# Sparse attention scores of two batches from f16 halves in 64x32 tiles of the array

## The chip, the cores and the metric

One core of one Trainium2 chip runs the whole kernel in one launch. The metric is device time in microseconds (us), the median of the runs shown; lower is better.

## The reference, cut to what matters

Block-sparse attention over 4 batches of 8 heads (768 rows, head size 64, blocks of 32 rows), then one feed-forward layer on the 3072 x 512 result:

```python
scores = np.matmul(q, k.transpose(0, 1, 3, 2)) / np.sqrt(64)
mask = (abs(blk_i - blk_j) <= 1) | first block | last block (rows and columns alike)
mask |= the 3 sampled key blocks of each query block
attn = softmax(np.where(mask, scores, -1e9))
x = np.matmul(attn, v)                      # then (3072, 512)
h = x @ w_in                                # 512 x 2048
out = (h * erf(softplus(h))) @ w_out        # 2048 x 512
```

A middle query block sees at most 8 key blocks of 32: its three neighbours, three sampled ones, the first and the last. The first and the last query block see all 24.

## The kernel before, in words

Everything is arranged around one loop of 96 feed-forward groups (line 985), eight to a chunk of 256 rows. A group on TensorE is 24 matmuls for `h` (`ff_first`) and 12 for `o` (`ff_second`, two groups late); its activation is five ScalarE passes (`ff_logs`), a VectorE step (`ff_power`), one more ScalarE pass (`ff_exp`), and three VectorE steps that also make f16 halves (`ff_gate`, in the next step).

The attention of later rows is laid between the groups: 64 **units**, 16 to a batch, at most one to a step, in five or six of every eight steps (`until`, line 984). Of a batch's units ten are "m" (four middle query blocks of four heads), four are "f" (the first and last query block against all keys, two heads each), and two "e" (the two query blocks left over). With n the number of a unit in its batch, n = 0 to 9 are the m units. A unit takes `scores` on TensorE, `soft_max` on VectorE (a maximum per row and group), `soft_exp` on ScalarE (four exponentials, one f16 copy), `soft_low` on VectorE (the lower f16 half), and `soft_turn` (transposes by DMA, from the SP queue). Two units later `values` multiplies by V on TensorE in 128x32 tiles of the array, `norm` divides on VectorE, and for every second unit `turn` makes halves of x.

Each engine works in the order in which the program issues (`InOrder`, line 49). Within a step that is: h of this group; its ScalarE logs; values; gathers; scores; gate of the last group; norm; o; the row maximum; the next queries; power; exponentials; stores; turn; the low half and the transposes; then `behind` (line 822), the preparation of the next batch. The score tile has one buffer, `h` three.

Scores now are f32 for all batches. A head pair's queries are laid into `qm` with zeros, so that 128 rows of the array hold two heads; each query block is a 64-column tile. `scores` (line 568) makes, for an m unit, four matmuls of the end keys (64 columns, 128-column tiles, two query blocks at once) and eight of near and sampled keys (192 columns, 64-column tiles). TensorE runs every f32 matmul as two instructions.

Preparation of batch b+1 in `behind`: keys are loaded (`load_k`, n = 0, 2, 4, 6) and laid into blocks by GpSimd (`order_k`, n = 1, 3, 5, 7); values are loaded, squared on ScalarE (n = 2, 4), scaled by a power of two (n = 5), split into f16 halves by ScalarE and VectorE (n = 5, 6, 8, 9) and written to a table in DRAM, from which SP gathers blocks. Key blocks of the sampled numbers are gathered by GpSimd copies (`gather`). Queries are laid out by two VectorE copies (`order_q`, n odd).

Of the kernel before, what the change touches and what calls it, by code (L numbers as in the profile page):

```python
# [42 lines left out]
def sparse_attention_moe(ctx: ExitStack, tc: tile.TileContext, qT, kT, v, sampled, w_in, w_out, out):  # L43
# [56 lines left out]


    NKEY = 2 * (NB + 1)
    keys = cp.tile([P, NKEY + KGS * NR, HP * BLOCK], F32, tag="keys", name="keys")
    kring = iter(range(B * NM))

    def key_blocks(b):
        return keys[:, b % 2 * (NB + 1) : (b % 2 + 1) * (NB + 1)]

    samp2 = at.tile([P, NB, NR, 2], I32, tag="xf", name="samp2", bufs=1)
# [4 lines left out]
    def load_k(b, pr):  # L114

        if b == 0:
            if pr < 3:
                kr = at.tile([P, 1024], F32, tag="pT", name=f"kr_{b}_{pr}", bufs=3)[:, :S]
            else:
                kr = at.tile([P, KT * 2 * VW], F16, tag="vn", name=f"kr_{b}_{pr}", bufs=1).bitcast(F32)[:, :S]  # L120
        else:
            kr = wi[:, NK * NG :, :].rearrange("p n c -> p (n c)")[:, :S]
        sp.dma_start(kr, kT[b, 2 * pr : 2 * pr + 2].rearrange("t d s -> (t d) s"))
        krs[b, pr] = kr
# [8 lines left out]


    qts = {}
    qm = cp.tile([P, HP, 4, 2, BLOCK], F32, tag="qm", name="qm")
    pool.memset(qm, 0.0)

# [12 lines left out]
    def order_q(b, t):  # L151
        qt = qts.pop((b, t)).rearrange("p r (j c) -> p r j c", c=BLOCK)
        copy = act.copy if b == 0 and t in (1, 2) else dve.tensor_copy
        for a in range(2):
            copy(qm[a * D : (a + 1) * D, :, :, a, :], qt[a * D : (a + 1) * D])

    QW = 4 * VW
# [47 lines left out]
    def pow2_scale(whole, tag):  # L205

        m = st.tile([P, 1], F32, tag="m", name=f"m_{tag}", bufs=1)
        dve.tensor_scalar_max(m, whole, 1e-37)
        e = st.tile([P, 1], I32, tag="e", name=f"e_{tag}", bufs=1)
        dve.tensor_scalar(e, m.bitcast(I32), 24, None, ALU.logical_shift_right)  # L210
        s = st.tile([P, 1], F32, tag="s_" + tag[:2], name=f"s_{tag}", bufs=1)
        inv = st.tile([P, 1], F32, tag="i_" + tag[:2], name=f"i_{tag}", bufs=1)
# [3 lines left out]
        return s, inv  # L216

# [188 lines left out]

    def weight_tile(name, n):
        return cp.tile([P, n + 2, 512], F32, tag=name, name=name)

    NG = DFF // 512  # L410
    wi = weight_tile("wi", NK * NG)
    wo = weight_tile("wo", NF)
    wi16 = wi.rearrange("p n c -> p (n c)").bitcast(F16).rearrange("p (n c) -> p n c", c=1024)
# [99 lines left out]
    def soft_max(unit):  # L513

        s, groups, width = softs[unit]
        tag = "_".join(str(x) for x in unit)
        mx = st.tile([P, 4], F32, tag="mx", name=f"mx_{tag}")[:, :groups]
        dve.reduce_max(mx, s.rearrange("p (g w) -> p g w", w=width), AX.X)
        nb = st.tile([P, 4], F32, tag="nb", name=f"nb_{tag}")[:, :groups]
        dve.tensor_scalar(nb, mx, -1.0 / math.sqrt(D), P_SHIFT * math.log(2.0), ALU.mult, ALU.add)  # L520
        softs[unit] += (nb,)

    def soft_exp(unit):
# [3 lines left out]
        n = groups * width  # L527
        pf = at.tile([P, 1024], F32, tag="pf", name=f"pf_{tag}", bufs=1)[:, :n]
        for g in range(groups):
            c = slice(g * width, (g + 1) * width)  # L530
            act.activation(pf[:, c], s[:, c], AF.Exp, bias=nb[:, g : g + 1], scale=1.0 / math.sqrt(D))
        p2 = at.tile([P, 2048], F16, tag="p2", name=f"p2_{tag}", bufs=2)[:, : 2 * n]
# [33 lines left out]
    pts = {}  # L566

    def scores(unit):
        kind, b, n = unit[0], unit[1], unit[2:]
        tag = "_".join(str(x) for x in unit)  # L570
        s = ps_s.tile([P, 1024], F32, tag="s", name=f"s_{tag}")
        if kind == "m":
# [15 lines left out]
        elif kind == "e":  # L588
            (quad,) = n
            s3 = s.rearrange("p (r w) -> p r w", r=HP)  # L590
            for r in range(2):
                pr = 2 * quad + r
                q_ = qm[:, pr, :2].rearrange("p j a c -> p (j a c)")
                pe.matmul(s3[:, r, 192:], q_, end_keys(b, pr), start=True, stop=True)
                for j in range(2):
# [16 lines left out]
    def values(b, t, quad):  # L612
        po = ps_po.tile([P, 4, D + 1], F32, tag="po", name=f"po_{b}_{t}_{quad}")
        for hl in range(4):
# [5 lines left out]
            for x, ln in ((0, 0), (0, 1), (1, 0)):  # L620
                for half in range(2):
                    for j in range(4):
                        if t < MT:
                            pT = pts["m", b, t, quad][:, ((j // 2) * 2 + r) * 4 + x * 2 + half]
                            col = (j % 2) * 64 + a * 32
                            vg = vb[:, slot_of[b, 1 + 4 * t + j]]
                        elif j in (1, 2):
                            pT, col = pts["e", b, quad][:, r * 4 + x * 2 + half], (j - 1) * 64 + a * 32
                            vg = vb[:, slot_of[b, NB - 4 + j]]
# [4 lines left out]
                if t == MT:  # L634
                    for k in range(KT):
                        for j in (0, 3):
                            pT, col = pts["f", b, pr][:, x * KT + k], (0 if j else 64) + a * 32
                            w = slice(c, c + D + 1) if ln == 0 else slice(c + D + 2, c + VW)
# [172 lines left out]
    def next_queries(m):  # L811

        b, n = divmod(m, per)
        if n < 10 and n % 2 == 1:
            order_q(b, n // 2 + 1)
            if n < 9:
                load_q(b, n // 2 + 2)
        if n == per - 1 and b + 1 < B:
            order_q(b + 1, 0)
            load_q(b + 1, 1)  # L820

    def behind(m):

        b, n = divmod(m, per)
        if b + 1 < B:
            c = b + 1
            if n == 10:
                load_q(c, 0)
            k = n if b else 2 * (n - 10) if n > 9 else -1
            if k in ((1, 3, 5, 7) if b else (2, 4, 6, 8)):  # L830
                order_k(c, (k - 1) // 2)
            if k in (0, 2, 4, 6):
                load_k(c, k // 2)
            if k == 8:
                have_k.add(c)
            if b == 0:
                n -= 4
            if n in (1, 7):
                load_v(c, 0)
            if n == 3:  # L840
                load_v(c, 1)
            if n in (2, 4):
                square_v(c, n // 2 - 1)
            if n == 5:
                scale_v(c)
            if n in (5, 6):
                split_v(c, 1, n - 5)
            if n in (8, 9):
                split_v(c, 0, n - 8)
            if n == 9:  # L850
                have_v.add(c)

# [228 lines left out]
```

## Time and profile before

| | us |
|---|---|
| median of 3 runs | 847.46 (846.92, 847.46, 854.24) |
| the profiled execution | 845.28 |
| its span, first to last instruction | 843.5 |
| TensorE busy | 742.9 (88%) |
| ScalarE busy | 601.3 (71%) |
| VectorE busy | 554.4 (66%) |
| GpSimd busy | 125.9 (15%) |
| mean granted TensorE clock | 0.939 of 2.4 GHz |

In the names of the profile, PE is TensorE, PEld its weight loads, ACT ScalarE, DVE VectorE, POOL GpSimd, SPq the queue of DMAs that SyncE issues. All instructions go through one helper and so bear one line number; they are told apart by tile names: `s_m`, `s_f`, `s_e` are the scores of the three kinds, `pf` and `p` their exponentials and f16 halves, `pT` the transposed halves, `po` the product with the values, `vn` the f16 halves of the values, `vj` the squares of the values.

### The profile page before, as it was taken

How to read it: one execution, taken by the hardware profiler on the slowest of the kernel's cores; microseconds unless marked ns; L12 is line 12 of the kernel's file. 1: busy time of each engine (PE TensorE's matmuls, PEld its weight loads, DVE VectorE, ACT ScalarE, POOL GpSimd, SP SyncE). 2: the span in 40 equal slices, each digit the busy share in tenths (PEclk: the TensorE clock that was granted, in tenths of full speed). 3: DMA queues.
4: the chain of work that ended last, by engine and by line, in shares of the span. 5: the costliest groups of instructions: out<-in, count | busy, mean ns of one | idle time of the engine just before them, and what ended most of it. 6: DMA issues, size and time to landing. Idle time of an engine off the chain costs nothing.

```text
span 843.5 us, 24600 instructions
## 1 busy us (share of the span) xinstructions
PE 742.9 (88%) x10044; PEld 513.2 (61%) x10044; DVE 554.4 (66%) x977; ACT 601.3 (71%) x999; POOL 125.9 (15%) x344
## 2 busy tenths in 40 slices
PE   1364647899999999989999999999999999999997
PEld 1253424666666676656777666566676776666664
DVE  3985696887665766755667676757576767655454
ACT  4654657987766777866778777868577777777774
POOL 5521111001222221000202221000111100000000
PEclk9865867989989999999999999999999999999999
DMA  8999853797788687741597798633476858111000
GB/s 326 269 276 317 220 138 78 171 208 171 178 220 205 185 206 201 185 89 44 135 218 186 198 194 189 161 84 82 106 175 175 175 109 196 39 32 40 1 26 26
DMA packets 199922, 131.48 MB, mean 156 GB/s; under 512 B 144000, under 2 KB 167168, under 8 KB 199808
## 3 DMA queue, kind: packets, MB, share of 16 engines
q1 hardware_dynamic: 196384, 118.10, 57.3%
q0 software_dynamic: 3424, 11.80, 4.1%
q8 instruction: 79, 1.29, 0.6%
q14 instruction: 35, 0.29, 0.1%
HBM read 83.88 MB, written 12.95 MB: 115 GB/s over the span
## 4 chain that ended last, share of the span: by engine, by line
PE 47%; DVE 19%; DMA 13%; ACT 12%; issue 5%; SPq 3%; POOL 0%; ACTq 0%; POOLq 0%
PE h L59 18%; PE o L59 17%; PE s_m L59 6%; DMA vb<-vtab 5%; PE po L59 3%; DVE g L59 3%; DVE q L59 3%; DMA vtab<-vn 3%; SPq L59 3%; DVE mx_m L59 3%; ACT x L59 3%; DMA vraw<-in_v_dram 3%; ACT pf_m L59 2%; ACT q L59 2%; DVE p_m L59 2%
## 5 line engine op out<-in xcount | busy, mean ns | idle before, releaser
L59 PE MATMUL h<-xT,wi 128*128 128x256 f16 x2304 | 274.9, 277 | 12.4 <-ACT wi L59 5.4
L59 PE MATMUL o<-wo,g 128*128 128x512 f16 x1152 | 270.5, 385 | 4.0 <-ACT wo L59 2.3
L59 PEld LDWEIGHTS <-wi 128*128 128x128 f16 x2304 | 227.7, 99 | 64.1 <-ACT wi L59 6.7
L59 PEld LDWEIGHTS <-g 128*128 128x128 f16 x1152 | 110.5, 99 | 138.2 <-issue 22.1
L59 ACT ACTIVATE x<-x 128x512 f32<-128x512 f32 x288 | 181.5, 630 | 9.2
L59 POOL COPY keys<-keys 128x128 f32 x264 | 92.9, 404 | 296.6 <-PE s_m L59 190.1
L59 PE MATMUL s_m<-keys,qm 128*64 128x192 f32 (+1 forms) x960 | 117.1, 344 | 4.5 <-ACT pf_m L59 3.7
L59 ACT ACTIVATE pf_m<-s_m,nb_m 128x256 f32<-128x256 f32 x160 | 62.8, 475 | 70.4 <-DVE nb_m L59 65.5
L59 DVE SCALAR_TENSOR_TENSOR q<-x,q 128x512 f32<-128x512 f32 x96 | 66.8, 696 | 62.5 <-ACT x L59 61.2
L59 PEld LDWEIGHTS s_m<-keys,qm 128*64 128x64 f32 (+1 forms) x960 | 90.9, 171 | 18.4 <-ACT pf_m L59 4.7
L59 ACT ACTIVATE x<-h,isg 128x512 f32<-128x512 f32 x96 | 65.3, 680 | 40.7 <-PE h L59 40.3
L59 ACT ACTIVATE q<-q 128x512 f32<-128x512 f32 x96 | 59.5, 619 | 29.8 <-DVE q L59 29.8
L59 DVE SCALAR_TENSOR_TENSOR q<-q,h 128x512 f32<-128x512 f32 x96 | 65.5, 682 | 22.6 <-ACT q L59 21.9
L59 DVE TENSOR_TENSOR p_m<-pf_m,p_m 128x1024 f16<-128x1024 f32 x40 | 49.1, 1228 | 32.3 <-ACT p_m L59 32.3
L59 DVE SCALAR_TENSOR_TENSOR g<-q,g 128x512 f16<-128x512 f32 x96 | 67.1, 699 | 3.3
L59 DVE TENSOR_REDUCE mx_m<-s_m 128x4 f32<-128x1024 f32 x40 | 48.8, 1220 | 31.1 <-PE s_m L59 31.1
L59 ACT ACTIVATE q<-x 128x512 f32<-128x512 f32 x96 | 60.5, 630 | 3.0
L59 PE MATMUL po<-vb,pT_m 128*32 128x65 f16 (+1 forms) x3840 | 44.1, 203 | 16.7 <-DMA vb<-vtab 10.2
L59 PEld LDWEIGHTS <-pT_m 128*32 128x32 f16 x3840 | 37.7, 99 | 27.7 <-DMA vb<-vtab 11.7
L59 DVE TENSOR_TENSOR x<-xf,x 128x512 f16<-128x512 f32 x24 | 16.9, 703 | 42.8 <-ACT x L59 42.8
L59 DVE TENSOR_SCALAR g<-q 128x512 f16<-128x512 f32 x96 | 41.5, 433 | 3.3
L59 ACT ACTIVATE p_m<-pf_m 128x1024 f16<-128x1024 f32 x40 | 42.3, 1057 | 1.3
(111 smaller groups left out, 544.1 us busy)
## 6 DMA issues: line engine op xcount, KB each, us to landing
vb<-vtab SPq DMA_DIRECT2D x280, 65.0 KB, 2.8
vb<-vtab SPq DMA_DIRECT2D x32, 390.0 KB, 4.0
vraw<-in_v_dram SPq DMA_DIRECT2D x10, 768.0 KB, 5.0
vtab<-vn SPq DMA_DIRECT2D x16, 390.0 KB, 4.9
vb<-vtab SPq DMA_DIRECT2D x12, 520.0 KB, 5.0
qt<-in_qT_dram SPq DMA_DIRECT2D x20, 256.0 KB, 3.7
out_dram<-wo SPq DMA_DIRECT2D x20, 256.0 KB, 3.5
vb<-vtab SPq DMA_DIRECT2D x36, 130.0 KB, 2.9
```

Source lines behind the costliest of these rows:

```text
L59: done = call(*args, **kwargs)
```

## The change

For batches 0 and 1 one thing differs: the end keys are multiplied block by block, eight matmuls in 64-column tiles in place of four in 128-column tiles (likewise in the e units).

For batches 2 and 3 keys and queries are scaled by a power of two, taken from the sum of their squares, and split into two f16 halves, which take the room of the f32 value. A score is the sum of three products, high by high, high by low and low by high. There are no zeros any more: the two heads of a pair lie in the two row halves of the array. The near and sampled keys of an m unit are 48 matmuls of 192 columns in 64x32 tiles, the end keys 12 of 64 columns in 64x128 tiles; an f unit is 12 matmuls in 64x64 tiles, an e unit 12 and 24. The two heads of an m or e unit are 512 columns apart in the score tile, those of an f unit lie in the same columns of the two partition halves.

The preparation of batches 2 and 3 (in `behind`, during batches 1 and 2) changes: keys and queries are first loaded raw and squared on ScalarE (eight squares, five more loads), a scale is made, keys are loaded again and split by ScalarE and VectorE (n = 5 to 8) where GpSimd laid them out; queries are split by ScalarE and VectorE in place of two VectorE copies. The steps for the values move to later n. Preparation of batch 1 stays as it was (`behind_whole`).

```diff
+    def split_k(b, pr):
+        ...
+        hi, lo = kx[:, :NB, 0, c], kx[:, :NB, 1, c]
+        act.activation(hi, kr, AF.Copy, scale=s)
+        dve.scalar_tensor_tensor(lo, kr, s, hi, ALU.mult, ALU.subtract)
+        if pr == HP - 1:
+            pool.tensor_copy(key_blocks(b)[:, NB], key_blocks(b)[:, 0])
+    def raw_k(b, pr):
+        sp.dma_start(spare_wi, kT[b, 2 * pr : 2 * pr + 2].rearrange("t d s -> (t d) s"))
+    def raw_two(b, key, pr):
+        place = ld.tile([P, H // 2, KT * D], F32, tag="vraw", name=f"{key}raw_{b}_{pr}", bufs=1)
+        ...
+        sp.dma_start(place, x[b, 2 * pr : 2 * pr + 4].rearrange("(r t) d s -> (t d) r s", t=2))
+    def square_raw(b, key, pr):
+        ...
+        act.activation(junk, raws.pop((b, key, pr)), AF.Square, accum_out=qksq[b][:, n : n + 1])
+    def bound_qk(b):
+        dve.tensor_reduce(top, qksq.pop(b).rearrange("p (x n) -> p x n", n=HP), AX.X, ALU.add)
+    def scale_qk(b):
+        pe.matmul(whole, one.to_broadcast([P, P]), qktop.pop(b), start=True, stop=True)
+        qkscale[b] = pow2_scale(whole, f"q{b}")
+        ...
+    def split_q(b, t):
+        hi, lo = qh[:, t % 2, 0], qh[:, t % 2, 1]
+        act.activation(hi, qt, AF.Copy, scale=s)
+        dve.scalar_tensor_tensor(lo, qt, s, hi, ALU.mult, ALU.subtract)
...
+    THREE = ((0, 0), (0, 1), (1, 0))
+    def half_products(outs):
+        for n, (x, y) in enumerate(THREE):
+            for out, a, lhs, rhs in outs:
+                rows = slice(a * D, (a + 1) * D)
+                pe.matmul(out, lhs(rows, x), rhs(rows, y), start=n == 0, stop=n == 2)
+    def half_scores(unit):
+        ...
+        if kind == "f":
+            for c, e in ((0, 512), (512, S)):
+                half_products([(s[a * D : (a + 1) * D, c:e], a, ...) for a in range(2)])
+        ...
+        for r, o, out in turns:
+            half_products([(out[o : o + whole, a, 192:256], a, ...) for a in range(2)])
+        for r, o, out in turns:
+            for j in range(blocks):
+                for a in range(2):
+                    place = out[o + c : o + c + BLOCK, a, :192]
+                    outs.append((place, a, queries(pr, c, c + BLOCK), keys_near(first + j, pr)))
+            half_products(outs)
     def scores(unit):
+        if b >= FB:
+            half_scores(unit)
+            return
...
-                for g in range(2):
-                    q_ = qm[:, pr, 2 * g : 2 * g + 2].rearrange("p j a c -> p (j a c)")
-                    pe.matmul(s4[:, g, r, 192:], q_, end_keys(b, pr), start=True, stop=True)
+                for j in range(4):
+                    o = slice((j % 2) * 64, (j % 2) * 64 + 64)
+                    q_ = qm[:, pr, j].rearrange("p a c -> p (a c)")
+                    pe.matmul(s4[o, j // 2, r, 192:], q_, end_keys(b, pr), start=True, stop=True)
...
     def behind(m):
         if b + 1 < B:
             c = b + 1
+            if c < FB:
+                behind_whole(c, b, n)
+                return
+            if n == 0:
+                raw_k(c, 0)
+                raw_two(c, "k", 1)
+            if n == 1:
+                for pr in range(3):
+                    square_raw(c, "k", pr)
+                raw_k(c, 3)
+                raw_two(c, "q", 0)
+            if n == 2:
+                square_raw(c, "k", 3)
+                square_raw(c, "q", 0)
+                square_raw(c, "q", 1)
+                load_k(c, 0)
+                raw_two(c, "q", 2)
+            if n == 3:
+                square_raw(c, "q", 2)
+                square_raw(c, "q", 3)
+                bound_qk(c)
                 load_v(c, 0)
+            if n == 4:
+                scale_qk(c)
+                square_v(c, 0)
                 load_v(c, 1)
             if n == 5:
+                square_v(c, 1)
+            if 5 <= n < 9:
+                split_k(c, n - 5)
+                if n < 8:
+                    load_k(c, n - 4)
+            if n == 6:
                 scale_v(c)
+            if n in (6, 7):
+                split_v(c, 1, n - 6)
+            if n == 7:
+                load_v(c, 0)
             if n in (8, 9):
                 split_v(c, 0, n - 8)
```

## Rows read from the trace of the kernel before

**Rows 1.** The page, part 1: busy time and share of the span.

```profile
PE 742.9 (88%) x10044; PEld 513.2 (61%) x10044; DVE 554.4 (66%) x977; ACT 601.3 (71%) x999; POOL 125.9 (15%) x344
```

**Rows 2.** Busy time by stage: length, PE, PEld, DVE, ACT, POOL, clock, DMA, GB/s.

```profile
216.50:322.80 106.30, 101.71 (x1516) 72.02 (x1515) 67.75 (x125) 75.07 (x132) 25.26 (x68) 0.95 0.82 200
395.00:508.00 113.00, 110.88 (x1624) 78.93 (x1622) 75.07 (x136) 86.27 (x150) 22.49 (x59) 1.00 0.76 185
573.80:687.00 113.20, 111.66 (x1622) 79.30 (x1621) 73.60 (x130) 83.59 (x142) 15.15 (x48) 0.98 0.66 146
```

**Rows 3.** TensorE's timeline, one unit step of batch 3 (start, length, ..., count).

```profile
627.84 2.78 PE L59 MATMUL h<-xT,wi 128*128 128x256 f16 x24
630.56 0.96 PE L59 MATMUL po<-vb,pT_m 128*32 128x65 f16 x96
631.44 2.56 PE L59 MATMUL s_m<-keys,qm 128*128 128x64 f32 x24
633.93 2.76 PE L59 MATMUL o<-wo,g 128*128 128x512 f16 x12
636.53 2.78 PE L59 MATMUL h<-xT,wi 128*128 128x256 f16 x24
```

**Rows 4.** The chain of waits, an f and an e unit of batch 2.

```profile
542.59 1.29 PE s_f L59 x4
...
557.87 1.68 PE s_e L59 x12
```

**Rows 5.** VectorE's and ScalarE's timelines between neighbouring units of batch 3.

```profile
638.26 1.23 DVE L59 TENSOR_TENSOR p_m<-pf_m,p_m 128x1024 f16<-128x1024 f32 x1 [2.19 <-ACT p_m L59]
642.76 1.23 DVE L59 TENSOR_REDUCE mx_m<-s_m 128x4 f32<-128x1024 f32 x1 [0.75 <-PE s_m L59]
...
639.35 0.69 ACT L59 ACTIVATE x<-h,isg 128x512 f32<-128x512 f32 x1 [0.61 <-PE h L59]
642.06 0.63 ACT L59 ACTIVATE x<-x 128x512 f32<-128x512 f32 x1
645.93 1.06 ACT L59 ACTIVATE p_m<-pf_m 128x1024 f16<-128x1024 f32 x1
```

**Rows 6.** ScalarE's timeline in batch 2: units n = 1, 2, then 7, 8.

```profile
418.69 1.06 ACT L59 ACTIVATE p_m<-pf_m 128x1024 f16<-128x1024 f32 x1
428.20 1.06 ACT L59 ACTIVATE p_m<-pf_m 128x1024 f16<-128x1024 f32 x1
...
491.16 1.06 ACT L59 ACTIVATE p_m<-pf_m 128x1024 f16<-128x1024 f32 x1
504.03 1.06 ACT L59 ACTIVATE p_m<-pf_m 128x1024 f16<-128x1024 f32 x1
509.25 1.12 ACT L59 ACTIVATE vn<-vraw,s_v 128x384 f16<-128x384 f32 x2 [3.65 <-issue]
```

**Rows 7.** The tile p_m in batch 3: count, first and last start.

```profile
L59 ACT ACTIVATE p_m<-pf_m x10: 1056/1057/1057, 582.0 to 696.2; 128x1024 f16<-128x1024 f32 x10
```

**Rows 8.** Groups by shape: total busy us, mean ns of one.

```profile
L59 ACT ACTIVATE vj<-vraw 128x768 bf16<-128x768 f32 x14 | 11.7, 835 | 1.3 <-DMA vraw<-in_v_dram 1.2
L59 ACT ACTIVATION_READ_ACCUMULATOR vj<-vraw 128x1 f32 x14 | 2.6, 186 | 0.0
L59 DVE SCALAR_TENSOR_TENSOR vn<-vraw,s_v,vn 128x384 f16<-128x384 f32 x28 | 16.1, 620 | 16.1 <-ACT vn L59 16.1
L59 DVE SCALAR_TENSOR_TENSOR wi<-wi,s_wi 128x1024 f16<-128x1024 f32 x8 | 10.4, 1303 | 1.9 <-ACT wi L59 1.9
```

**Rows 9.** ScalarE's waits, 446 to 508 us: total, times, longest.

```profile
ACT vn L59 <- DVE i_v L59: 2.4, 1, 2.4
```

**Rows 10.** SP's queue, batch 3: one gather of value blocks.

```profile
632.73 7.19 SPq L59 DMA_DIRECT2D vb<-vtab  x14
```

**Rows 11.** TensorE's timeline where it stood still in batch 3.

```profile
593.02 0.37 PE L59 MATMUL po<-vb,pT_f 128*32 128x64 f16 x13 [1.54 <-issue]
593.33 3.81 PE L59 MATMUL s_m<-keys,qm 128*128 128x64 f32 x24
```

More of the change, by code (lines that the diff above doesn't have):

```diff
@@ new lines, in half_scores, with queries, keys_at, keys_near @@
+    def half_scores(unit):
+        kind, b, n = unit[0], unit[1], unit[2:]
+        tag = "_".join(str(x) for x in unit)
+        s = ps_s.tile([P, 1024], F32, tag="s", name=f"s_{tag}")
+        t = n[0] if kind == "m" else MT
+        q = qh[:, t % 2]
+        base = b % 2 * (NB + 1)
+        def queries(pr, c, e):
+            return lambda rows, x: q[rows, x, pr, c:e]
+        def keys_at(first, last, pr, step=1):
+            c = slice(pr * BLOCK, (pr + 1) * BLOCK)
+            return lambda rows, x: halves_of_keys[rows, base + first : base + last : step, x, c]
+        def keys_near(i, pr):
+            return lambda rows, x: half_near(rows, b, i, pr, x)
+        if kind == "f":
+            (pr,) = n
+            for c, e in ((0, 512), (512, S)):
+                half_products(
+                    [
+                        (s[a * D : (a + 1) * D, c:e], a, queries(pr, 2 * BLOCK, P), keys_at(c // BLOCK, e // BLOCK, pr))
+                        for a in range(2)
+                    ]
+                )
+            softs[unit] = (s[:, :S], 1, S)
+            return
+        if kind == "m":
+            quad = n[1]
+            s4 = s.rearrange("p (a r w) -> p a r w", a=2, r=2)
+            first, blocks, turns = 1 + 4 * t, 4, [(r, 0, s4[:, :, r]) for r in range(2)]
+            softs[unit] = (s, 4, 256)
+        else:
+            (quad,) = n
+            s3 = s.rearrange("p (a w) -> p a w", a=2)[:, :, :256]
+            first, blocks, turns = NB - 3, 2, [(r, r * D, s3) for r in range(2)]
+            softs[unit] = (s3, 2, 256)
+        whole = blocks * BLOCK
+        for r, o, out in turns:
+            pr = 2 * quad + r
+            half_products(
+                [
+                    (out[o : o + whole, a, 192:256], a, queries(pr, 0, whole), keys_at(0, NB, pr, NB - 1))
+                    for a in range(2)
+                ]
+            )
+        for r, o, out in turns:
+            pr = 2 * quad + r
+            outs = []
+            for j in range(blocks):
+                c = j * BLOCK
+                for a in range(2):
+                    place = out[o + c : o + c + BLOCK, a, :192]
+                    outs.append((place, a, queries(pr, c, c + BLOCK), keys_near(first + j, pr)))
+            half_products(outs)
@@ L592, in scores @@
                 pr = 2 * quad + r
-                q_ = qm[:, pr, :2].rearrange("p j a c -> p (j a c)")
-                pe.matmul(s3[:, r, 192:], q_, end_keys(b, pr), start=True, stop=True)
+                for j in range(2):
+                    o = slice(j * 64, j * 64 + 64)
+                    q_ = qm[:, pr, j].rearrange("p a c -> p (a c)")
+                    pe.matmul(s3[o, r, 192:], q_, end_keys(b, pr), start=True, stop=True)
                 for j in range(2):
@@ L850, in behind @@
             if n == 9:
+                have_k.add(c)
                 have_v.add(c)
```

124 lines of the change are left out of this document (89 added, 35 removed).

## The prediction

> **What bounds the kernel now.** I read the page first: TensorE is busy 88% of the span, the next engine 71% [rows 1]. A share over the whole says little, so the second view is busy time by stage, over the m units of batches 1, 2 and 3 [rows 2]: TensorE is busy 96% to 99% of each, ScalarE 71% to 76%, VectorE 64% to 66%. By this view TensorE is the bound, and the reader is tempted to take off what the change takes off TensorE.
>
> The third view, the timelines, shows what comes next. TensorE takes 8.69 us for a step with a unit: 2.72 for h, 0.88 for the values, 2.49 for the scores, 2.60 for o [rows 3]. A step without a unit is two stretches of 6144 columns, 2.60 each: 5.20. Beside it runs a loop through VectorE and ScalarE: lower half of unit n, gate, division, maximum of unit n+1 (VectorE), four exponentials and the f16 copy (ScalarE), then the lower half again. Between neighbouring units it took 8.73, from 638.26 to the end of the copy at 646.99, and in it VectorE waited for the scores 0.75 [rows 5]. The loop alone is thus 8.0: it lies 0.7 below TensorE's 8.69. With a step without a unit between, the copies of n = 7 and 8 end 12.87 apart [rows 6], against TensorE's 8.69 + 5.20 = 13.89. With the turning of x between neighbours, n = 1 to 2, it is 9.51 [rows 6], already above TensorE's 8.69. So TensorE may become faster by about 0.7 to 1.0 per unit before the loop is the bound, and what lengthens the loop costs at once.
>
> **What TensorE saves.** The f unit streams 768 columns in 1.29 [rows 4]: 1.68 ns a column in f32, against 2.60 / 6144 = 0.42 in f16 [rows 3]. An e unit has half of an m unit's matmuls but four changes of tile shape where m has two: 2 x 1.68 - 2.49 = 0.87 is six changes, 0.15 each [rows 3, 4]. Of the m unit's 2.49, near keys are 8 x 192 x 1.68 ns, two at once, 1.29; changes 0.30; end keys the remaining 0.90.
>
> After, in batches 2 and 3: the 48 near matmuls run in six sets of eight tiles, 192 x 0.42 = 81 ns a set, 0.48. For the end keys the nearest row is the values, 96 matmuls of 65 columns in four tiles in 0.88 [rows 3]: 37 ns a set, six sets 0.22. With two changes, 1.00, so 1.49 saved. No row shows tiles in row halves. Bounds: at the values' pace of 9.2 ns per matmul the unit is 60 x 9.2 ns + 0.30 = 0.85; with the two row halves one after the other it is 1.71. I take 1.00, since the values' four tiles already run side by side. An e unit is 0.48 + 0.22 + 0.30 = 1.00, saving 0.68; an f unit 3 x 768 x 0.42 ns + 0.15 = 1.12, saving 0.17, or at the other bound 2.09, costing 0.80. Per batch 14.9 + 1.4 + 0.7 = 17, for two 34.
>
> On f the Trainium skill speaks against the change: TensorEngine Tiling (Array Packing), Gotcha 1: PSUM Pressure, says that different row tiles cannot access the same PSUM bank at once. The f unit's two heads go to the same columns; by that rule it takes the 2.09, and the sum rises by 8 x 0.97 = 7.8. No row here shows it either way.
>
> In batches 0 and 1 the end keys become 16 instructions of half the tile width, two at once as the near keys are: half of 0.90, and one change fewer, 0.60 saved per m unit, 0.67 per e unit (three changes and half of its 0.45), 7.3 per batch. If the weight loads don't run side by side it is only the changes, 0.15 and 0.45. In all TensorE sheds up to 49.
>
> The same skill has a second rule against it: TensorE: Matmul & The Clock Gate, in the section on the 56 ns, gives 25 ns as the least from one matmul's start to the next. By it the m unit would be 60 x 25 ns + 0.30 = 1.80. The values' 9.2 ns [rows 3] contradict that floor for tiles side by side, so I keep 1.00; by 1.80 the sum would rise by about 5, since the loop hides the rest.
>
> **What the loop gives back.** Batch 3 has no preparation behind it. Its ten copies lie 114.2 apart from first to last [rows 7]. By the loop: neighbours 9.5 + 8.0 + 8.0, six with a free step at 12.9, and 1.6 for a double set of values (0.9) and a store on ScalarE (0.7): 104.5. The standstill of 1.54 and the slower scores behind it, 3.81 against 2.56 [rows 3, 11], come on top if they stay: 107.3. Saved 7 to 10, I take 8; the f and e units save their 2.0: **-10**.
>
> In batches 1 and 2 ScalarE and VectorE prepare the next batch. A square is 0.835 + 0.186 = 1.02; a split on ScalarE the same 0.84; the lower half of 768 columns lies between 0.62 for 384 and 1.30 for 1024, 1.03 [rows 8]. Between two copies ScalarE has the last exponential, 0.5, and the logs, 3.3 (639.35 to 642.69), and VectorE 5.3 up to the maximum's end [rows 5]; ScalarE thus has 1.4 free between neighbours, and none with a free step between, where logs and power lie on the path. Step by step in batch 2, against now:
> - n = 0: TensorE binds here, two sets of values: -1.5.
> - n = 1: three squares and the turn's copy: 0.5 + 0.6 + 3.1 + 3.3 = 7.5 against VectorE's 9.5 - 2.7 = 6.8: +0.7.
> - n = 2: three squares for two of the values, a free step behind: +1.0. n = 3: two squares, likewise: +2.0. n = 4: the scale, three more one-column steps at 0.19 (the shortest row): +0.5.
> - n = 5: the wait of 2.4 for the values' scale [rows 9] and a split of 1.2 go, two squares and a split come: -0.5. n = 6: that wait comes here, covered in part, with a lower half of 1.03: +2.2. n = 7: lower halves of 1.03 and 2 x 0.62 where there were none: +2.3. n = 8: one more lower half, but the wait of 3.65 for the values' load [rows 6] shrinks, as the steps before it are longer: -1.5.
>
> That is +5.2; f and e units save 2.0: **+3**. In batch 1 six units follow each other without a free step, where ScalarE's 1.4 hides n = 3 wholly, and n = 0 saves 0.6: +4.1, less 1.3 for e: **+3**. Batch 0 is bound by the start; of its 7.3 I take **-2** (ends 0 and -7).
>
> Queries: two VectorE copies become one ScalarE and one VectorE pass beside the exponentials, nothing. GpSimd loses the laying out of keys; behind it waited nobody for long, nothing. Five more loads per batch stand on SP's queue ahead of the next gathers: 7.19 / 14 = 0.51 per issue [rows 10], 5 in all; between nothing and 5 I take **+2**. Cover for it is the two units between transposition and values.
>
> Sum: -10 + 3 + 3 - 2 + 2 = -4 against the profiled 845.3, 841.3. The median of the runs shown lies 2.2 above that execution: **843**.
>
> **Rivals.**
> TensorE is the only bound, the loop adjusts: 845.3 - 49 + 2.2 = 798. For it 96% to 99% busy; against it the 8.0, 9.51 and 12.87. Chance 0.10.
>
> The preparation hides: ScalarE is idle 31 and 27 in these stages of batches 1 and 2 [rows 2], the additions vanish, and their TensorE gains show for a third of 16.9 and 7.3: -10 - 6 - 2 - 2 = -20, 828. Against it the order on each engine: idle time lies ahead of the exponentials, the squares behind them. Chance 0.15.
>
> Slower: the raw loads come late. Each is issued behind a unit's transposes, and, where its place holds earlier data, behind the squares of that; one step later ScalarE stands at its square, with the logs, the exponentials, and so h's and the score tile's buffers behind it. The wait of 3.65 for the values [rows 6] is this mechanism. Ten such waits (n = 1 to 5, two batches), each 3.65 less 1.4 free, are 22: 865. It decides from six of the ten on, 13 above forecast. For it SP's issues back to back, 7.19 [rows 10]; against it most of the steps are 9 to 15 long. Chance 0.20.
>
> f's row halves exclude each other (the bound of 2.09): 843 + 6 = 849, since most of the f units lie where TensorE binds. Chance 0.05.
>
> The change not doing what it says, no tiles side by side: excluded by the values' row, within 0.02.
>
> **Numbers.** The forecast has 0.48; its own range is 833 to 853, a quarter of it below 839. A measurement of this kernel can tell about 1%, 8 us, from no change. Faster by more: 0.10 + 0.15 + 0.12 = 0.37. Slower by more: 0.20 and the 0.02 = 0.22. Within: 0.41. The range, 820 to 862, leaves out the first rival and the upper half of the third.
>
> **What would show it.** Right: scores of an m unit near 1.0, TensorE's busy share in batch 2's m units fallen to some 85%, the row maximum no longer waiting for scores, copies of neighbours 8.0 apart in batch 3, n = 6 and 7 of batches 1 and 2 over 2 longer. Wrong: ScalarE waiting for raw loads; an f unit of 2.1; neighbours under 8; or a TensorE that now stands still so often that its granted clock falls more than in [rows 2], each fall costing what the 3.81 shows [rows 11].

## The result, and the profile after

The changed kernel took 856.21 us (median of 18 runs, 850.69 to 862.82) against 847.38 of the kernel before: a ratio of 1.0097, 95% interval 1.0073 to 1.0121. It is slower by about 8 us where 843 and "no change that can be told" were forecast. The profiled execution took 852.04, its span is 850.0, four below the median.

Part 1 and part 4 of the page after:

```profile
PE 703.6 (83%) x11104; PEld 475.2 (56%) x11104; DVE 561.8 (66%) x987; ACT 636.2 (75%) x1051; POOL 117.6 (14%) x330
...
PE 33%; DVE 22%; ACT 21%; DMA 14%; issue 7%; SPq 2%; POOL 1%; ACTq 0%; POOLq 0%; DVEq 0%
```

TensorE has 39 us less to do than in [rows 1], and the kernel is slower. Its share of the chain that ended last is 33%, where it was 47% before.

Stages, cut at the ends of the f16 copies of n = 0 and n = 9 of each batch, show where (us, worked out from the starts of `p_m` in the timelines; the first stage is from the start to batch 1's n = 0, "f, e" runs to the next batch's n = 0):

| | start | m, batch 1 | f, e | m, batch 2 | f, e | m, batch 3 | rest |
|---|---|---|---|---|---|---|---|
| before | 225.8 | 111.6 | 67.0 | 117.4 | 61.4 | 114.2 | 146.2 |
| after | 230.6 | 118.8 | 60.0 | 128.8 | 59.6 | 107.5 | 144.6 |
| `ends_only` | 226.8 | 112.8 | 59.7 | 116.9 | 61.6 | 111.6 | 149.0 |
| `fixed_scale` | 229.3 | 115.7 | 61.1 | 120.7 | 58.7 | 108.2 | 144.5 |
| `no_loads` | 226.8 | 117.1 | 59.5 | 121.5 | 58.6 | 107.0 | 144.4 |

Batch 3 gains, as forecast; batch 2 loses 11.4 where 5.2 was forecast. Up to batch 1's n = 0 after and `ends_only` issue the same instructions, so of the 4.8 at the start 3.8 lie between executions, not in the program. The 67.0 of before is long for a reason of its own: TensorE stood 2.2 there without a semaphore, and its granted clock was 1.2 GHz from 376.0 to 382.8; after and `ends_only` have neither in that stage.

TensorE's timeline of unit steps in batch 3 after (start, length, ..., count), against [rows 3]:

```profile
637.39 2.78 PE L59 MATMUL h<-xT,wi 128*128 128x256 f16 x24
640.10 1.08 PE L59 MATMUL po<-vb,pT_m 128*32 128x65 f16 x96
641.12 0.97 PE L59 MATMUL s_m<-keys,qm 64*128 64x64 f16 x60
642.02 2.76 PE L59 MATMUL o<-wo,g 128*128 128x512 f16 x12
644.62 2.78 PE L59 MATMUL h<-xT,wi 128*128 128x256 f16 x24
```

From the scores' start to o's is 0.90, against 2.49 before. An f and an e unit in the chain after, against 1.29 and 1.68 of [rows 4]:

```profile
558.22 1.09 PE s_f L59 x12
...
573.60 0.63 PE s_e L59 x36
```

The stages of the m units of batches 1, 2 and 3 after (columns as in [rows 2]):

```profile
221.20:340.00 118.80, 102.41 (x1639) 71.25 (x1641) 75.61 (x141) 88.86 (x159) 21.82 (x62) 0.91 0.89 215
398.00:527.00 129.00, 112.41 (x2015) 74.13 (x2017) 82.03 (x149) 106.28 (x182) 17.82 (x52) 0.92 0.82 192
577.00:685.00 108.00, 98.75 (x1821) 67.62 (x1819) 72.43 (x124) 87.41 (x144) 14.96 (x48) 1.00 0.62 140
```

In batch 1's stage the DMA engines are at 0.89 and TensorE's granted clock at 0.91; in batch 2's 0.82 and 0.92. In batch 3's, where nothing is prepared, 0.62 and 1.00. ScalarE's timeline of the copies of batch 2, n = 0 to 8:

```profile
408.34 1.06 ACT L59 ACTIVATE p_m<-pf_m 128x1024 f16<-128x1024 f32 x1
427.98 1.06 ACT L59 ACTIVATE p_m<-pf_m 128x1024 f16<-128x1024 f32 x1
437.92 1.06 ACT L59 ACTIVATE p_m<-pf_m 128x1024 f16<-128x1024 f32 x1
453.45 1.06 ACT L59 ACTIVATE p_m<-pf_m 128x1024 f16<-128x1024 f32 x1
468.06 1.06 ACT L59 ACTIVATE p_m<-pf_m 128x1024 f16<-128x1024 f32 x1
477.29 1.06 ACT L59 ACTIVATE p_m<-pf_m 128x1024 f16<-128x1024 f32 x1
493.29 1.06 ACT L59 ACTIVATE p_m<-pf_m 128x1024 f16<-128x1024 f32 x1
505.96 1.06 ACT L59 ACTIVATE p_m<-pf_m 128x1024 f16<-128x1024 f32 x1
521.40 1.06 ACT L59 ACTIVATE p_m<-pf_m 128x1024 f16<-128x1024 f32 x1
```

| from n to n + 1 | 0 | 1 | 2 | 3 | 4 | 5 | 6 | 7 | 8 |
|---|---|---|---|---|---|---|---|---|---|
| before | 15.37 | 9.51 | 14.74 | 12.98 | 9.12 | 16.48 | 9.64 | 12.87 | 16.64 |
| after | 19.64 | 9.94 | 15.53 | 14.61 | 9.23 | 16.00 | 12.67 | 15.44 | 15.77 |
| difference | +4.3 | +0.4 | +0.8 | +1.6 | +0.1 | -0.5 | +3.0 | +2.6 | -0.9 |
| forecast | -1.5 | +0.7 | +1.0 | +2.0 | +0.5 | -0.5 | +2.2 | +2.3 | -1.5 |

From n = 1 on the steps of the preparation cost what was forecast, within 0.8 each. The step from n = 0 to 1 is the one that came out far off: TensorE was to save 1.5 there, and 4.3 were lost. Its timeline and three stretches of it (columns as before):

```profile
416.17 0.19 PE L59 MATMUL po<-vb,pT_e 128*32 128x64 f16 x2
421.83 0.90 PE L59 MATMUL po<-vb,pT_f 128*32 128x65 f16 x25
422.66 1.59 PE L59 MATMUL s_m<-keys,qm 64*128 64x64 f16 x60
424.19 3.75 PE L59 MATMUL o<-wo,g 128*128 128x512 f16 x12
```

```profile
416.30:419.40 3.10, 0.20 (x23) 0.07 (x8) 0.69 (x1) 2.55 (x5) 0.00 (x0) 1.00 0.99 327
419.40:421.80 2.40, 0.00 (x0) 0.00 (x0) 0.00 (x0) 0.00 (x0) 0.00 (x0) 0.50 0.11 33
421.80:426.20 4.40, 4.38 (x93) 2.61 (x94) 2.57 (x6) 0.19 (x1) 1.79 (x8) 0.50 0.54 156
```

In the middle of the values' product TensorE stands for 5.5 us. No semaphore holds it; VectorE does little in it, and in its last 2.4 us none of the engines listed does anything. The granted clock is at half, 1.2 GHz, from 419.4 to 426.2, and the scores take 1.59 where they take 0.97. A raw load of batch 3's keys was issued just before, the second of the tile `kraw`:

```profile
L59 SPq DMA_DIRECT2D kraw<-in_kT_dram x2: 420/429/438, 235.1 to 412.8; - x2
...
DMA to landing us min/median/max: 5.4/5.9/6.5
```

Issued at 412.8, it landed at 419.3, within the standstill; until then the DMA engines were 0.99 busy, after it 0.11. That is a suspicion, and the experiments are on it.

### The profile page after: what moved, and what is told of

Read it like the earlier page. It is cut to its first block, busy times and chain, and to the rows that moved or that the text cites. A ratio compares the mean times of both kernels' runs of the same rounds, so it can differ in the third digit from the quotient of the medians.

```text
span 850.0 us, 26780 instructions
## 1 busy us (share of the span) xinstructions
PE 703.6 (83%) x11104; PEld 475.2 (56%) x11104; DVE 561.8 (66%) x987; ACT 636.2 (75%) x1051; POOL 117.6 (14%) x330
## 2 busy tenths in 40 slices
DMA packets 202138, 137.90 MB, mean 162 GB/s; under 512 B 144160, under 2 KB 167328, under 8 KB 202016
## 3 DMA queue, kind: packets, MB, share of 16 engines
q1 hardware_dynamic: 198592, 124.39, 60.7%
## 4 chain that ended last, share of the span: by engine, by line
PE 33%; DVE 22%; ACT 21%; DMA 14%; issue 7%; SPq 2%; POOL 1%; ACTq 0%; POOLq 0%; DVEq 0%
PE o L59 13%; PE h L59 13%; ACT x L59 6%; DMA vb<-vtab 4%; DVE g L59 4%; ACT pf_m L59 4%; DVE q L59 4%; ACT q L59 4%; DVE mx_m L59 3%; PE po L59 3%; DMA vtab<-vn 3%; DMA vraw<-in_v_dram 2%; DMA qraw<-in_qT_dram 2%; PE s_m L59 2%; DVE p_m L59 2%
## 5 line engine op out<-in xcount | busy, mean ns | idle before, releaser
L59 PE MATMUL h<-xT,wi 128*128 128x256 f16 x2304 | 276.6, 278 | 13.9 <-ACT wi L59 7.7
L59 PE MATMUL o<-wo,g 128*128 128x512 f16 x1152 | 275.5, 389 | 8.8 <-ACT wo L59 3.2
L59 PE MATMUL s_m<-keys,qm 64*32 64x192 f16 (+3 forms) x1840 | 74.5, 270 | 21.6 <-POOL keys L59 8.6
L59 ACT ACTIVATE q<-q 128x512 f32<-128x512 f32 x96 | 59.5, 620 | 29.9 <-DVE q L59 29.9
L59 PE MATMUL po<-vb,pT_m 128*32 128x65 f16 (+1 forms) x3840 | 47.0, 205 | 29.1 <-DMA vb<-vtab 20.3
L59 PEld LDWEIGHTS <-pT_m 128*32 128x32 f16 x3840 | 39.8, 101 | 40.6 <-DMA vb<-vtab 22.1
L59 DVE TENSOR_REDUCE mx_m<-s_m 128x4 f32<-128x1024 f32 x40 | 48.6, 1216 | 12.9 <-PE s_m L59 12.8
L59 ACT ACTIVATE pf_m<-s_m,nb_m,s_q 128x256 f32<-128x256 f32 x80 | 38.6, 563 | 23.3 <-DVE nb_m L59 23.0
L59 ACT ACTIVATE pf_m<-s_m,nb_m 128x256 f32<-128x256 f32 x80 | 31.3, 474 | 32.1 <-DVE nb_m L59 27.9
L59 PEld LDWEIGHTS s_m<-keys,qm 128*64 128x64 f32 x640 | 37.3, 163 | 16.3 <-POOL keys L59 5.7
```

Of the source, the lines that this page charges most:

```text
L59: done = call(*args, **kwargs)
```

## The experiments

Theory when they began: what was not in the sum sits in the preparation of batches 2 and 3. The candidates are the raw loads, the squares on ScalarE, the factors read from a tile, GpSimd's place in the chain, and the 60 small matmuls. All were timed in five rounds. A difference between two kernels is the difference of their ratios to the kernel before, times 847.4; its 95% interval, from the two intervals, is about 4 us each way.

**`ends_only`**: f32 in all batches, end keys block by block. **`last_batch`**: halves in batch 3 alone.

```diff
-    FB = 2
+    FB = 4      # last_batch: 3
```

> All four batches keep f32 scores; only the end keys go block by block. Loop theory (VectorE and ScalarE bound the units, TensorE's savings mostly hidden): 842 to 847, since 0.6 us a unit is shed by an engine with little say. Start theory (the changed kernel's first unit of batch 1 came 4.8 us later in its profile, and the end keys are the only change that early): 850 to 853, with the first h no earlier than 93 us. If neither, it equals the kernel before within 0.3%.

> f16 scores and their preparation for batch 3 alone; batch 2 keeps f32 scores, batch 1 has no new preparation. Loop theory: batch 3 keeps its gain (the ten copies 107 apart instead of 114, 2 more in f and e), batch 2's m units bear the preparation once and take 10 to 12 more than the 117 of before: 845 to 851. If the cost lies in f16 scoring itself (more instructions on TensorE, slower exponentials) and not in the preparation, half of the difference to before stays: 850 to 853 with both batches a little longer.

842.02, ratio 0.9933 (0.9905 to 0.9962), and 846.26, 0.9981 (0.9950 to 1.0012). The ends alone are a gain of 5.7, and TensorE's busy time in `ends_only` falls from 742.9 to 713.6: 29.3, the forecast 7.3 for each of four batches. Where the 5.7 lies the traces don't show: of the 5.0 between the two profiled executions more than all, 7.3, is the long stage of before at batch 1's f and e units. Halves in batch 3 alone give back 4.1 of the gain: batch 3's m units gain 4.8 more and the rest 4.0, but batch 2's m units, beside which batch 3 is prepared, take 128.0 against 116.9. The loss is in the preparation, not in the scores: where it runs, beside f32 scores, the step from n = 0 to 1 of batch 2 takes 5.1 more than before.

**`fixed_slope`**: the factor of the maximum and of the exponential as a constant.

```diff
-        slope = expscale[unit[1]][:, 0:1] if unit[1] >= FB else 1.0 / math.sqrt(D)
+        slope = 1.0 / math.sqrt(D) / (1024.0 if unit[1] >= FB else 1.0)
```

> As the changed kernel, but the factor of the exponentials and of the row maximum is a number in the instruction and not read from a tile (the scale is 32 for these inputs, so the values agree). The profile after shows 563 ns for one exponential against 474 with a number. Loop theory: 4 x 0.09 = 0.36 us comes off each of 20 m units, up to 7: 849 to 853. If TensorE or its instruction supply is the bound: no change, 856.

852.74, 1.0064 (1.0032 to 1.0096): 2.8 less than after, not clear of zero. The trace shows the size. The tile `pf_m` after, by shape (count, min/median/max ns):

```profile
L59 ACT ACTIVATE pf_m<-s_m,nb_m x80: 453/475/487, 23.1 to 347.8; 128x256 f32<-128x256 f32 x80
L59 ACT ACTIVATE pf_m<-s_m,nb_m,s_q x80: 554/564/572, 406.4 to 703.6; 128x256 f32<-128x256 f32 x80
```

and in `fixed_slope`:

```profile
L59 ACT ACTIVATE pf_m<-s_m,nb_m x160: 453/473/486, 23.1 to 702.3; 128x256 f32<-128x256 f32 x160
```

An exponential that reads its factor from a tile takes 90 ns more; four follow each other in the loop that binds, 20 units: about 7 of ScalarE's time, of which part shows.

**`fixed_scale`**: `fixed_slope` with the splits' factor 32 as a constant of these inputs, so no raw loads, squares or scale.

```diff
-        s = qkscale[b][0][:, 1:2]
+        s = 32.0
...
-            if n == 0:
-                raw_k(c, 0)
-                raw_two(c, "k", 1)
...
```

> As fixed_slope, and the split too takes the number 32, so that the raw loads, the 16 squares and the scale of keys and queries are left out. Loop theory: n = 1 to 4 of batches 1 and 2 lose 0.7 + 1.0 + 2.0 + 0.5 twice over, some 6 to 8 us, on top of fixed_slope's gain: 841 to 846. If the raw loads' traffic is what delays TensorE's instruction fetches (standstills without a semaphore rose from 5 to 22 us): those fall back towards 5 to 10 in all, and the time to 838 to 845. If the price lies in the splits and the SP queue: 849 or more.

839.42, 0.9902 (0.9866 to 0.9939), 13.7 less than `fixed_slope`. TensorE's busy time is 694.5: 48.4 less than before, the forecast's 49. With the scale's preparation out, the forecast's sum is about right in total: -4 less its own 2 for loads and at least 4.2 for squares (n = 1 to 4 of batch 2) is -10; measured -8.3. The expectation that the standstills without a semaphore would nearly vanish failed: the largest such wait in batch 2's stage, of the weight loads, falls from 29.5 to 20.4, not to 5 or 10.

**`no_squares`**: `fixed_slope` with the factor 32; the raw loads stay, nothing reads them. **`no_loads`**: likewise with the factor 32; the squares and the scale stay, on a tile that is there, and no raw loads.

```diff
-        act.activation(junk, raws.pop((b, key, pr)), AF.Square, accum_out=qksq[b][:, n : n + 1])
+        raws.pop((b, key, pr))                                       # no_squares
...
-        sp.dma_start(place, x[b, 2 * pr : 2 * pr + 4].rearrange("(r t) d s -> (t d) r s", t=2))
...
-            raws[b, key, pr + r] = place[:, r]
+            raws[b, key, pr + r] = spare_wi                          # no_loads
...
```

> fixed_slope (852.7) without the squares and the scale, but with the five more loads per batch, whose data nobody reads. Between fixed_slope and fixed_scale (839.4) lie 13.3 us. If ScalarE's time in the loop is the price (my forecast's terms, 4.2 in a batch): most goes with the squares, 841 to 845. If the loads' traffic and SP's issue slots are the price: 848 to 852.

> fixed_slope with the squares, taken of a tile that is already there, and the scale, without the five loads. The mirror of no_squares: ScalarE's time gives 849 to 852; traffic and SP give 840 to 844. If neither, and the price is ScalarE waiting for the loads to land, both kernels come out near fixed_scale, 840 to 844.

851.89, 1.0066 (1.0036 to 1.0096): without the squares nothing is won. 840.99, 0.9941 (0.9910 to 0.9973): without the loads 10.4 are. The same from the other side: `no_squares` differs from `fixed_scale` by the loads, 13.9; `no_loads` from `fixed_scale` by the squares and the scale, 3.3. So the ten raw loads cost 10 to 14. By stages the price lies where the loads do: batch 1's and batch 2's m units take 122.0 and 126.5 in `no_squares` against 115.7 and 120.7 in `fixed_scale`, 6 more in each, and no other stage differs by more than 1.4.

TensorE's waits in batch 2's stage (us in total, times, longest). After:

```profile
PEld L59 <- issue: 29.5, 56, 5.5
PE po L59 <- issue: 5.3, 1, 5.3
```

`no_squares`:

```profile
PEld L59 <- issue: 23.0, 35, 5.5
PE po L59 <- issue: 5.4, 1, 5.4
```

`no_loads`:

```profile
PEld L59 <- issue: 16.8, 30, 2.0
PE po L59 <- issue: 1.8, 1, 1.8
```

The standstill in the values' product is 5.3 and 5.4 with the loads and 1.8 without, and the step from n = 0 to 1 of batch 2 is 15.1 in `no_loads` (copies at 402.33 and 417.42) against 19.6; before, `PEld <- issue` was 4.7 in this stage. The step tells them apart in all sixteen kernels: with full raw loads there (after, `fixed_slope`, `no_squares`, `last_batch` and `f32_loads`, whose scores there are f32) it takes 4.2 to 5.1 more than before, in the ten others between 1.3 less and 1.0 more.

**`small_loads`**: `no_squares` with 96 of the 768 columns in each raw load: as many issues, an eighth of the bytes. **`f32_loads`**: f32 scores in all batches and unread full raw loads; **`f32_order`**: the same without the loads. Both have the changed order of the preparation, with GpSimd laying out the keys at n = 5 to 8.

```diff
-        sp.dma_start(place, x[b, 2 * pr : 2 * pr + 4].rearrange("(r t) d s -> (t d) r s", t=2))
+        sp.dma_start(place[:, :, :96], x[b, 2 * pr : 2 * pr + 4].rearrange("(r t) d s -> (t d) r s", t=2)[:, :, :96])
...                                                                  # raw_k likewise
-                split_k(c, n - 5)
+                order_k(c, n - 5)                                    # f32_loads, f32_order, with FB = 4
```

> no_squares (851.9) with the same ten loads at the same places, of 96 columns of the 768: as many issues on SP, an eighth of the bytes. If the price of the loads is SP's time to issue and its order: 849 to 853. If it is the bytes on the DMA engines, behind which value gathers and TensorE's instruction fetches land late: 840 to 844, and the standstill of 5.5 at n = 1 of batch 2, which all four kernels with full loads for batch 3 show at 410 to 417 us, shrinks to about 2.

> f32 scores in all batches (as ends_only, 842.0), the order of the changed preparation for batches 2 and 3 with GpSimd laying out the keys, and the ten full loads, read by nobody. If the loads cost by traffic alone, whatever TensorE computes: 851 to 854. If they cost only together with f16 scores, whose 120 instructions a unit drain TensorE's instruction stream faster: 842 to 846.

> f32 scores everywhere as in ends_only, the changed order of the preparation as in f32_loads (keys laid out by GpSimd at n = 5 to 8, the steps for the values later), but none of the ten raw loads. If the loads alone made f32_loads dear (856.2 against 842.0 of ends_only), this run lies near ends_only, 842 to 845, and its m stages of batches 1 and 2 near 113 and 117. If the later order of the preparation did it, it lies near f32_loads, 853 to 857. In between, the two share the 14.

`small_loads`: 842.16, 0.9962 (0.9935 to 0.9988), 8.8 less than `no_squares`. Its wait:

```profile
PEld L59 <- issue: 19.5, 33, 2.0
...
PE po L59 <- issue: 1.7, 1, 1.7
```

So most of the price is the bytes, and not the issues on SP's queue that the forecast priced. `small_loads` is still 5.1 above `fixed_scale`, just clear of zero, so that the issues and the last eighth of the bytes may well cost up to the 5 that the forecast allowed; the bytes come on top. `f32_loads`: 856.17, 1.0136 (1.0098 to 1.0175); `f32_order`: 848.09, 1.0029 (1.0007 to 1.0052). The loads cost 9.1 here too. The other 8.1 of `f32_loads` over `ends_only` is the order of the preparation with GpSimd's laying out: the expectation that the loads alone made it dear was wrong.

TensorE's waits in the whole of `f32_loads`:

```profile
PE po L59 <- DMA vb<-vtab: 19.8, 11, 5.8
...
PE po L59 <- DMA pT_m<-p_m: 13.0, 6, 3.9
```

and of `f32_order`:

```profile
PE po L59 <- DMA vb<-vtab: 15.2, 8, 5.9
...
PE po L59 <- DMA pT_m<-p_m: 9.2, 4, 3.4
```

With f32 scores the loads show as 8.4 more of waiting for gathered value blocks and transposes and as a standstill without a semaphore at n = 0 to 1 of batch 2, 3.5 against 1.3, and TensorE's busy time stays (716.3 and 716.4). With halves it doesn't: 702.9 in `no_squares`, 694.9 in `small_loads`, 694.5 in `fixed_scale`. There the loads show as longer standstills without a semaphore and as matmuls at the lower clock. Within the intervals the price is the same with both; that it is paid by whatever TensorE needs next is a reading, not a test.

**`early_squares`**: after, with batch 3's raw loads, squares and scale at n = 10 to 14 of batch 1, among the f and e units.

```diff
...
+            if c == 2:
+                raw_steps(3, n - 10)
+                raw_steps(2, n)
...
```

> The changed kernel (856.2), with the raw loads, squares and scale for batch 3 one batch earlier, at n = 10 to 14 of batch 1, where the DMA engines are busy 45 to 52% and not 80 to 89%; those of batch 2 stay. If the place of the loads makes the price, half of 11 goes: 849 to 852, with batch 2's m units near 121 instead of 128.8 and no 5.5 standstill at n = 1. If the amount makes it: 855 to 857.

851.56, 1.0056 (1.0027 to 1.0085): 3.5 less than after. Batch 2's m units fall from 128.8 to 125.6, the f and e units of batch 1 before them rise from 60.0 to 63.1. The standstill at n = 0 to 1 is gone but for 1.9, as expected; the 121 expected for the stage is not reached. The 3.5 are hardly clear of zero, and squares and scale moved with the loads, so the run shows only that the move does not make them free.

**`one_product`**: `fixed_scale` with the product of the high halves alone (two of three products are left out).

```diff
-    THREE = ((0, 0), (0, 1), (1, 0))
+    THREE = ((0, 0),)
```

> fixed_scale (839.4) with the high-by-high product alone, leaving out the other two: 20 matmuls instead of 60 in an m unit, TensorE busy some 0.45 us less in each of 20. Loop theory: TensorE waits for the loop in these units, so the time stays within 2 us, 837 to 841. Instruction theory (TensorE runs dry, 12 standstills without a semaphore that end 1.2 to 1.5 us after a fetch landed, 19 us in fixed_scale): they fall to the 5 to 9 of the kernels with f32 scores, and the time by 4 or more, 835 or less.

834.34, 0.9862 (0.9819 to 0.9905), 3.4 less than `fixed_scale`, not clear of zero; TensorE's busy time falls by 9.2. By these numbers most of a further saving on TensorE is hidden by now, as the loop of the prediction would have it. The run does not settle between the two theories of its expectation: the time came out where the one on instructions had it, and TensorE's standstills of over 1 us without a semaphore are 4 in place of 8 (from 225 to 700 us), but the weight loads' wait on `issue` in batch 2's stage stays, 20.2 and 20.4.

**`one_memset`**: `fixed_scale` where one tile `vn` is kept and its ones are written once, so that GpSimd need not wait for the table's write ahead of its key copies. **`late_split`**: `fixed_scale` with the keys loaded and split at n = 9 to 13. **`late_once`**: both.

```diff
+        if (0, 0, 0) in kept:                                        # one_memset, late_once
+            vns[b, quad, half] = kept[0, 0, 0]
+            return
...
+        if b:
+            kept[0, 0, 0] = vn
...
-            if 5 <= n < 9:
-                split_k(c, n - 5)
+            if 10 <= n < 14:                                         # late_split, late_once
+                split_k(c, n - 10)
+            if 9 <= n < 13:
+                load_k(c, n - 9)
...
```

> fixed_scale with the ones beside the value halves written once, in a tile kept for all batches, so GpSimd no longer stands at a memset (n = 7) that waits for the table write of n = 6 while the key copies of n = 8 queue behind it. In the profile after, the scores of n = 8 waited for keys 5 us in batches 1 and 2. GpSimd theory: 2 to 3 us off each of the two, 833 to 836. Loop theory (VectorE's lower halves set n = 7 to 8 anyway, 2.3 over): 838 to 840.

> one_memset (838.7) with the key loads and splits moved from n = 5 to 8 to n = 9 to 13, into the f and e units. My forecast's n = 6 to 8 (2.2 + 2.3 + 1 in each of two batches) should come back, less what the f and e units must bear: 831 to 835. If VectorE's lower halves were hidden behind waits for keys and values anyway: 837 to 840.

> fixed_scale (839.4) with the key loads and splits moved to n = 9 to 13, behind the steps for the values, and the vn tile written with its ones for every half as before. If the splits' place beside the values' steps costs the m stages (fixed_scale 115.7 and 120.7), both fall by 2 to 3 and the time to 834 to 837. If the GpSimd write of the ones behind the wait for the table is what late_once got rid of, the time stays at 839 to 840.

838.65, 0.9908 (0.9878 to 0.9937); 837.39, 0.9897 (0.9857 to 0.9938); 837.43, 0.9904 (0.9871 to 0.9937). None can be told from `fixed_scale`. Yet the wait for GpSimd's key copies did shrink. Scores of m units in `fixed_scale` (busy, mean ns | idle before):

```profile
L59 PE MATMUL s_m<-keys,qm 64*32 64x192 f16 (+3 forms) x1840 | 72.6, 270 | 18.8 <-issue 7.6 <-POOL keys L59 7.5 <-ACT pf_m L59 3.7
```

and in `late_split`:

```profile
L59 PE MATMUL s_m<-keys,qm 64*32 64x192 f16 (+3 forms) x1840 | 70.6, 265 | 15.0 <-issue 7.9 <-ACT pf_m L59 3.9 <-POOL keys L59 3.1
```

The wait went from 7.5 to 3.1 and nothing came of it in the time that the runs can show. The m units of batches 1 and 2 did get shorter, 113.1 and 115.5 against 115.7 and 120.7, and what followed took most of it up: batch 2's f and e units take 62.8 against 58.7, batch 3's m units 110.0 against 108.2. These three and `fixed_scale` beat both kernels by about 1% and 2%, as long as a constant scale may be used; `ends_only` keeps the inputs free and beats before by 0.7%.

## Why the prediction was wrong

**The step that failed** is "five more loads per batch ... between nothing and 5 I take +2". It priced a load by its issue on SP's queue, 0.51 from [rows 10], put its bytes at nothing, and named the two units between transposition and values as cover. Measured, the loads cost 9 to 14 (three pairs of kernels, about 4 us each way; `no_squares` against `fixed_scale` and the pair with f32 scores differ by the loads alone), and leaving seven eighths of their bytes out takes back 8.8. The row that spoke against it was in hand: the DMA engines at 0.82 and 0.76 in these stages [rows 2]. Ten loads are 6.3 MB more (137.90 moved in all against 131.61 in `no_loads`), put into the two busier of the three stages. Against a forecast of -4 and +8 measured, the 7 to 12 above this term are most of the 12 missed.

**Not in the sum at all**: the exponential's factor, 90 ns each, some 3 by `fixed_slope`. The change's code shows it, no row of before did, and it should have been bounded. The Trainium skill has this price: ScalarE: Activation LUTs, section What ACT_TABLE_LOAD costs, gives about 93 ns for each operand of one column read from a tile. The trace agrees: 564 against 475 ns.

**TensorE's terms were right.** m unit 1.00 forecast, 0.90 measured; f 1.12 and 1.09; e 1.00 and 0.63, so e was 0.4 too dear; in all 49 forecast and 48.4 in `fixed_scale`. The two rules of the Trainium skill that spoke against the change are not borne out here, for tiles side by side. By the Trainium skill's TensorEngine Tiling (Array Packing), Gotcha 1: PSUM Pressure, the f unit would take 2.09: it takes 1.09, with both heads in the same columns. By the 25 ns floor of the Trainium skill's TensorE: Matmul & The Clock Gate, in its section on the 56 ns, 60 matmuls would take 1.5 without the changes: they start within 0.90, 15 ns each.

**The loop and the preparation** were about right. Batch 3: 8 for the m units and 2.0 for f and e forecast, 6.7 and 1.6 measured. Copies and a row maximum of batch 3, ScalarE's and VectorE's timelines after:

```profile
634.41 1.06 ACT L59 ACTIVATE p_m<-pf_m 128x1024 f16<-128x1024 f32 x1
647.52 1.06 ACT L59 ACTIVATE p_m<-pf_m 128x1024 f16<-128x1024 f32 x1
655.82 1.06 ACT L59 ACTIVATE p_m<-pf_m 128x1024 f16<-128x1024 f32 x1
...
643.99 1.21 DVE L59 TENSOR_REDUCE mx_m<-s_m 128x4 f32<-128x1024 f32 x1
```

With a free step between them copies lie 13.1 apart, 12.9 forecast; neighbours 8.3, 8.0 forecast, and the slower exponentials are 0.36 of that (8.0 in `fixed_scale`, without them); the other such pair took 9.3. The maximum has no wait for the scores left, 0.75 in [rows 5]. Batch 2: n = 1 to 8 sum to +7.1 measured and +6.7 forecast; n = 0 is the loads', though without them it gains 0.3 (`no_loads`) and not 1.5. There is luck in the match: the exponentials are in the 7.1 and not in the 6.7, and taking squares and scale out gives back only 3.3 in all (`no_loads` against `fixed_scale`), since without them n = 5 costs 2.4 where -0.5 stood. Batch 1's m units came to +7.2 where 4.1 stood. Its f and e units came to -7.0 where -1.3 stood, and to the same 59.7 in `ends_only`, so the halves have no part in it. Most of it is the standstill in before: the 2.2, and half of the 6.8 us at the lower clock, in which TensorE was busy throughout, make 5.6 by estimate. The -2 for batch 0 didn't come: the start is 1.0 longer in the profiled execution of `ends_only` than in that of before.

**The rival of the late loads** gave 865 and the right sign, but not for its reason. ScalarE's squares waited for their loads 2.6 in total, all of it for queries, not 22. The tile `qraw` after (what its engine sat idle for; then the load's landing):

```profile
  DMA qraw<-in_qT_dram: 2.6, 3
...
DMA to landing us min/median/max: 5.5/5.8/6.1
```

and the square that the chain leads through, in ScalarE's timeline:

```profile
440.81 0.84 ACT L59 ACTIVATE j_q<-qraw 128x768 bf16<-128x768 f32 x1 [0.50 <-DMA qraw<-in_qT_dram]
```

The chain of waits puts 6.10 us on this load (434.63 to 440.73), because it released the square last; ScalarE had other work until 0.50 before. A piece of the chain is no price: `no_squares` has no such wait and is as slow as `fixed_slope`.

**What would make it wrong** had one sentence for what happened: a TensorE that stands still so often that its clock falls. Of batches 1 and 2 that came true, 0.95 and 1.00 to 0.91 and 0.92. It had no chance and no time of its own.

**Left open.** How the price with halves divides between standstills, the lower clock behind them, and late gathers: no kernel took one of them away alone. Of the standstill at n = 0 to 1 of batch 2 the loads make some 3.5, 5.3 against 1.8. The granted clock was at half, in the m stages of batches 1 and 2 together, for 41.0 us in after, 37.5 in `no_squares` and 20.5 in `fixed_scale` (before 10.2); at most half of the 17.0 between `no_squares` and `fixed_scale` can be lost time. Batch 1's waits for gathered values are 8.8 where they were 3.4 before, but 5.7 of it without any raw load, in `fixed_scale` (`vb`, waits of `po` in its stage, after):

```profile
PE po L59 <- DMA vb<-vtab: 8.8, 6, 5.4
```

## What to carry to other kernels

Price an added transfer by its bytes against the busy share of the DMA engines in the very stage where it lands, not by its issue alone; here, at 0.76 and 0.82, 6.3 MB cost 9 to 14 us through other work that waited. When the bound engine is only a tenth above a loop through the others, take the cheap saving first (the ends block by block gained 5.7 by four more matmuls a unit) and count what the larger one needs in preparation. A scale that data must be read twice for has that price too: as a constant it made the kernel 13.7 faster. Taking it from a load that is there anyway was not tried.

## What was not expected of the hardware

TensorE's own instructions came late. Part 3 of the page after (packets, MB, share of 16 engines):

```profile
q1 hardware_dynamic: 198592, 124.39, 60.7%
q0 software_dynamic: 3424, 11.80, 4.3%
q8 instruction: 87, 1.43, 0.7%
```

The instruction queue moves 87 packets where before it moved 79 (1.29 MB), among 198592 of data. Batch 2's `PEld <- issue` is 3.9 to 9.7 with f32 scores in it (4.7 before, 5.8 in `f32_loads`), 11.6 to 20.4 with halves and small or no loads in the stage, and 23.0 to 29.5 with full ones.

The DMA packets in the traces, with their times, tell more. Over all sixteen kernels, from 225 to 700 us, TensorE stood 93 times for over 1 us without a semaphore, and each time a packet of 16 KB of the instruction queue had ended 1.2 to 1.6 us before it went on; of 174 idle times of that length with another releaser 10 are so. So these standstills are waits for instructions. The one of 5.5 us ended at 421.82, behind a packet of 419.65 to 420.60, and that began once the raw load had landed (419.3) and the DMA engines had fallen from 0.99 to 0.11. In the five kernels with full raw loads at n = 0 of batch 2 (after, `fixed_slope`, `no_squares`, `f32_loads`, `last_batch`) this packet began 1.1 to 3.2 us into the standstill; in the other kernels that stand there it began before the standstill did. That it waited behind the data on the DMA engines fits all of this; no row shows the order on one engine, and so it is argued, not shown.

Also unexpected: with the standstill the granted clock falls to 1.2 GHz for 6.8 us. TensorE works in the last 4.4 of them, the scores taking 1.59 for 0.97 and o 3.75 for 2.76, which is some 2.2 us more lost, by estimate.
